# A new order for all instructions of a planned attention and expert kernel, with durations from the trace

## Chip, cores and metric

The kernel runs on one core of a Trainium2 chip. The metric is the device time in microseconds (us) of one execution; the median of several runs is given.

## The reference

A linear attention with a decaying state runs over 4 x 8 heads of 768 steps with 48 channels. Its outputs, taken as 3072 tokens of 384 channels, go through an RMS norm and a gated expert layer.

```python
for t in range(S):                       # attention, per batch and head
    state = alpha[t][:, None] * state + outer(k[t], v[t])
    y[t] = q[t] @ state
rms = sqrt(mean(x * x, axis=-1) + 1e-06)  # x: the 3072 x 384 outputs y
xn = x / rms * rms_g
g, val = xn @ w_gate, xn @ w_val          # 384 x 1536 each
out = (g * sigmoid(g) * val) @ w_out      # 1536 x 384
```

## The kernel before

The 3072 tokens are cut into 24 chunks of 128 (cc counts them; batch b is cc modulo 4). For a chunk, VectorE scans the decays forward and backward (`scan`, L644), with a reciprocal between the two (`rec`, L664), and multiplies k and q by the running products (`kh`, `qh`). TensorE then forms scores (`sc`, for the first four chunks `sc32`), VectorE masks them (`mask`, `near`), TensorE multiplies by v (`yv`, `y32`), sums the state (`u`) and gives the output y. The first four chunks start from no state and have short forms: `kp`, `kb`, `y32`, `ys32`. ScalarE squares y (`sq`, L951), POOL takes the power -1/2 (`pow`, L956), VectorE scales (`x32`, L965), TensorE transposes (`xp`, L972) and takes the rounded half off (`xneg`, L986), and ScalarE writes the two halves of x into tile xT.

Numbers are held as a 16-bit float and its 16-bit remainder, so one product of the experts is three matmuls with K = 128 for each of three parts. A step `mm` (L1152) is 9 matmuls into one PSUM bank. Tokens go in groups of 4, 2, 2, 4, 4, 4 and 4 chunks; for a group, each of 12 blocks of the hidden layer gets two `mm` steps (gate and value), then `silu` (ScalarE), `gate` (VectorE, L1169), `h_hi` (ScalarE, L496) and `h_lo` (VectorE, L1186). The output products are `po` (L1471) for the first five groups, and for the last two a scheme with seven products for eight, in steps of 9 matmuls (L1353), with `snap` (ScalarE, L1388) and `give` (VectorE, L1398 and L1400). The weights arrive as 8-byte words and are put together by `abs`, `shift`, `rest`, `wh` and `wl` (L518 to L540) before their first use.

Near the end a check is made: squares of recorded sums (ScalarE, `1e2`), a sum over partitions by TensorE (`1e3`), comparisons on VectorE (`1e4`), a second sum by TensorE (`1e5`) and a flag written by VectorE (`1e6`, L1654 and L1658). Every engine loads the flag into a register (L1676) and branches on it (L1677): one side is a general form of the kernel, the other issues the last three stores of the output, those of the last chunks, which SP holds back until then.

Nothing is ordered at run time: every step is an operation of a plan (about 1800, numbered as they are made), with an engine, a cost, the operations that it depends on and the buffers that it uses. ORDER lists the numbers in base 36. The planner walks through this list, gives each operation the earliest time by the costs, by its engine and by its inputs, picks the buffer that comes free first, and puts dummy matmuls (`warm`, L1591) where TensorE would wait by its reckoning in the first 45 us. Then all operations are issued in the order of these times, each engine's queue in this order. A transfer is issued by SP in its place of the same list.

Some numbers that are used below: `x`, `10`, `1m`, `1p` scans and `y` the reciprocal of chunks 1 and 2; `f`, `g`, `15` masks; `1r` a `qh`; `3b`, `3c` shift and join of the first weights, `39` their load, `3` the load of chunk 0's v; `j` y32 of chunk 0; `1f` x32 of chunk 1; `2p` ys32, `2r` squares, `2u` transpose and `2w` xneg of chunk 3; `6r` the gate product of block 4; `1dy` the last expert step of TensorE, `1dz` the `give` behind it, `1dv` the one before; `1dw` and `1e0` are SP's places for the last stores, which issue nothing there.

Of the kernel before, what the change touches and what calls it, by code (L numbers as in the profile page):

```python
# [62 lines left out]
COST = dict(
    scan=1.2, rec=0.19, kh=0.605, qh=0.337, kl=0.6, vl=0.47, ql=0.6, gd=0.09, sd=0.28, sl=0.27, mask=0.6,
    al=0.6, st=0.31, ss=0.12, x=0.46, xl=0.53, shift=0.525, rest=0.88, wl=0.87, ob=0.46, oba=0.385,
    dec=0.11, k16=0.62, v16=0.515, q16=0.62, s16=0.26, a16=0.515, sq=0.7, x16=0.52, st0=0.23,
    abs=0.91, odd=0.47, cnt=0.85, wh=0.845, pow=0.6, sc=1.03, scw=0.955, sc32=0.6, yv=0.665, yvw=0.548, y32=1.4, add=0.47, take=0.4, u=0.82, po=1.48, xp=0.46, kp=0.5,
    neg=0.3, hs=1.47, hsh=1.05, hsl=1.2, tw=0.95, ts=1.2, th=0.74, tl=0.87, p7=0.75, snap=0.33, give=0.36, wid=0.75, wneg=0.22, wl2=0.37, rgw=0.7, rgt=0.37, x32=0.53, xb=0.38, ys32=0.82, kb=0.53, near=0.34, xneg=0.22,
)
# [22 lines left out]
6s 45 6t 6o 9v 6x 6p 44 42 ai 6y 6z a3 6e 73 46 4a 6u 4f 47 6q 74 am 4b 75 6k a4 70 76 4c 77 79 an 71 48
4r 7a 7b 78 4d ao 7f 7g aq 7h 7c 9w a5 7l 7d ap 4g 7e 7m 4h 7n 4s 4i 7r 4e 4l 7o 4t 7p 7s ar 4j ay 72 4u
7t 6v 7x 7q 4v 4x 7u 9x 7v 7i as 4w 7y 7z az 4m 7w 4n 21 83 a7 4o au 4k 4p 53 ew 84 a6 b0 4y 80 a9 81 6w
89 85 4z a8 50 4q 5f 51 8a aa 54 86 8b 55 ab aw 56 8f 87 82 59 57 ib e0 ac ic 8g 8h 8c ax b1 52 8l at av
bg 5a ae 8m 5b 8n 88 8d 58 5g b2 5c 7j 8r 8i 5d 5l b4 8j b3 7k 8s b5 8k b6 b7 ad 8t 8o e2 im bh b8 af 8u
b9 5m 5h 8x 5i 8e 5r 5j 8y e1 5e 5k 8z 5n 5o 90 ed e3 5p 5x ex 91 8v dz ee e4 5s 5q 92 8p 5t ef ba 5u 93
e7 e5 5v 8w 94 5z 5y 5w 60 95 bk bb 61 8q 96 bi 62 eg 97 e6 ag eb e8 ah 98 bc ec bd e9 be eh 9b ey bf 9f
ez f0 ej 9c 9d kc ei el 9e 9g f1 9h en ea 99 fb f7 f3 9i f2 f4 j9 id f9 bm ev f5 fc bn f6 bo fd ie 9j ft
ig bs if ek bt em kd bu 9a iq f8 by bp ja ii ih bz c0 bj bv c4 ij c1 lc bl c2 fu jb bq io eo jc bw ir c5  # L100
c6 fa ep fe ca br c3 er eq cb c7 cc bx ik fx cg ip fy ch cd fv ce je jd cm ci jf ff cj il ck cn is fh j8
co c8 fg cs c9 fi cl ct es jo cp in cu fj jg cy fw jh cv cz p5 jm jp p6 ke cw d4 d0 cx d5 fk d6 cq cf jq
da d1 jk fl db et dc d2 cr eu kf dg d7 kh dh di kg jn dm dd kj de d3 ki fm dj dn kk fn fp q5 df dk le d8
do ji it lg dl iu lf fo kr d9 lh dp fq pg jj kl fr ds kp li fs iv dt iw ix k6 lj dq lk iy jr du 9k km dr
lr ph p7 ld dv x3 iz fz j0 dw jl j1 kq g1 p9 g0 ks j2 j4 p8 kn g5 pa js pc g7 pb g6 pd jt pi ra ls gb jv
g2 g8 jx g9 gc gd ju g3 gh ll ge q7 gi gj kt q8 lt ga k7 pj g4 gn lb j3 gk qa gl go gp q6 jw ka gt j5 pk
gm qc gf lu gu jy gv qd jz k8 gq gz j6 gr ln gg gs h0 k0 gw ku gx k2 h5 h1 gy q9 lm h6 h2 mb k9 h3 qb kv
h7 ko sa k1 h8 hb j7 kw k3 kx hc ky kb hd k4 lp hh l0 k5 kz he hi l1 hf pe hg hn lo h9 pf hj l2 pl hp qk
ho h4 pm l3 lq l4 ht hk hq lv rc hr hv l5 hu ha lw l6 hz rd ly lx hw lz l7 i0 hx m1 hl m0 l8 qe hy mc hs
re pn ql m2 l9 q4 i1 md m3 hm qg m4 rb qh sb m5 i2 qf dx la m6 mf m7 i5 rf i3 r4 qm qi rg po m8 m9 i6 me  # L110
ma pp rp pq i7 rh ps ri pr pu w3 rl x4 i8 pt qn sc pv i9 r5 sd se qj pw sl mh r6 rj sf sg mi mj rq mg rn
px ro mn sh r8 si y8 w5 i4 qo ia mp w6 mo sn qq mk w7 qs r7 sj rk mt py sp rm s9 qp mq qr w4 mu w8 mv xe
xf wa mz wb wi w9 mw qt n0 n1 sq mx qu mr x5 n5 ml mm q0 x6 n6 sk n7 ms sr t9 ss sm qv pz z8 n8 nb z9 n2
q1 rr wj n3 my q2 nc nd rs x8 x7 qw qx nh ne so nf rt nj qy ni ru rv rw ng n9 xa nn rx ry wc rz r0 ta xb
np r9 qz x9 no r1 nk n4 tb ya s0 nt r2 yb r3 s1 td yd yc wg nu nv s2 na s3 wh st s4 s5 nz te xg wd we nw
x2 nl yn nq xc o0 sv 13u o1 y9 xi xj nr nm nx yf o5 tc xd yg ye o6 wf 12v o7 za y2 sx ny ob o8 o2 o3 oc
od o4 s6 yo o9 ns oh s7 180 zb 176 oe s8 su oi sz sw q3 xh of oj oa xk zj og wk zc y3 zn sy ok y6 181 wl
182 183 zd on zf zo t0 177 y4 oo 16u 178 ze t1 zp t2 op yp zg 14t 12x wm 12z yj oq wn t3 184 zl wo t4
16x ot 185 12w 12y 16v wq zk t5 wp ou 13v ws 17l t6 zm 16w ov y7 zh wr or zi ol ow t7 om 130 os t8 wt oz
131 wu 107 wv 16y ww p0 zq 17u wx 132 17m zr yk 17n 17c p1 zs yq yh zt ox p2 yi zu yl z7 zv tf 17v 14u  # L120
xl ym 17f wy tg 133 th 13w p3 16z tl 13y 17w 17d 149 zw 170 15s ti 13x tm 13z tn tj y5 wz tr x0 17g to
17o 17h x1 zx ts tt 141 171 tp 142 179 154 140 tx tu 155 14v 15t p4 108 tz 13a 17e zy ty 17p zz 10b 172
17x 109 100 14w 101 u3 102 tq 103 17a u4 u5 13b 16r 14y 13c 17b tk xm tv u0 17q u9 17y 147 14a 173 xo
14x 17z u6 104 ua 148 xq xn ub 13d xp xs uf u7 xr u1 105 14b 16s 10a 17i xt 158 u2 106 ug xu 136 xv uh
u8 143 yr 144 174 ul uc 17r tw ud 14z xw um ui 175 xx xy 150 uj ys ur un 159 yu 17j 15a yt 186 uo us ut
14c 137 up 15b 151 163 15u 16t ux yv 15v yw 152 uq 15w uy 17k yx uz uk 156 10c v3 167 xz 153 187 uu 188
v0 yy y0 v4 145 168 y1 17s v5 164 yz uv z0 v9 ue 169 v1 uw z1 v6 14d z2 157 v7 15x vb va 15z v2 vf vc z3
v8 z4 vg 14f vd 17t ve vh 14e 16a 160 vi 189 165 14g 14h vl 14i vj 18a vk vm 166 14j vn 146 15y 18d vo
z5 z6 vr vp 161 vq 162 14k vs 14l 18b 14m 14n 16b 18c 14p vt 138 16d 16c 139 vu 16e 14o 16f 16g 134 16h
vx 14q 135 vv 14r vw 16i 18e vy 16j 16k 16l vz 16n 16m w0 16o 16p 13e w1 w2 10d 14s 13f 13g 13h 16q 13i  # L130
13j 10e 18f 13k 10f 18g 13l 10j 13m 13n 10g 13o 18l 10k 10l 13q 13p 18t 10s 10m 18u 10t 10u 18m 18v 13r
18w 10y 18n 10v 10p 15c 110 13s 10z 15e 13t 18o 15g 10w oy 15d 10h 117 10n 15i 10i 15f 111 10q 10o 118
112 10r 119 11d 11a 10x 15h 114 11e 11f 18p 115 15j 11g 11b 11m 18q 11h 11c 18r 113 11n 11o 11i 15k 18s
11s 116 11p 18h 11t 11u 11j 121 15l 18i 15m 11q 122 11v 18j 15o 123 15n 18k 11k 127 11r 1e1 11w 124 11l
128 129 11x 125 11y 12g 11z 12a 15p 120 12h 12i 12b 126 15q 12m 12d 15r 12j 12e 12n 12c 12o 12f 12k 18x
12p 18y 12s 12q 18z 190 12l 12t 12r 191 12u 193 192 194 196 195 197 199 198 19a 19b 19c 19f 19d 19e 19h
19i 19l 19j 19k 19m 19o 19n 19p 19q 19r 19u 19s 19t 19v 19z 19w 19g 1a0 19x 1a3 1a1 1a2 1a4 1a7 19y 1a5
1a8 1a9 1ad 1aa 1ab 1ac 1ae 1af 1am 1ag 1aj 1an 1ak 1ao 1as 1ah 1ap 1al 1at 1au 1aq 1b1 1av 1ay 1b2 1b3
1ar 1ai 1az 1b0 1b7 1b4 1b8 1b9 1bg 1ba 1bh 1bi 1bb 1aw 1bm 1ax 1bc 1bj 1bn 1bd 1bk 1bo 1be 1bv 1bf 1bw
1bp 1bl 1bq 1bs 1bx 1c1 1by 1bz 1c2 1c0 1c3 1br 1b5 1bt 1ca 1bu 1c4 1cb 1c7 1cc 1c8 1cg 1cd 1c5 1ce 1c6  # L140
# [1627 lines left out]
```

## Time and profile before

| what | value |
|---|---|
| median of 3 runs | 501.1 us (500.85 to 501.48) |
| span of the profiled execution | 500.0 us |
| its own time | listed by its span alone; 1.1 us less than the median of the runs |
| TensorE, matmul | 491.6 us busy, 98% |
| VectorE | 422.2 us busy, 84% |
| ScalarE | 277.0 us busy, 55% |
| POOL | 25.6 us busy, 5% |
| DMA | 65.22 MB, mean 130 GB/s |

The span reaches from the first to the last instruction of the profiled execution. Busy time counts arithmetic alone: loads into registers, branches and waits are not in it. Matmuls overlap in time, so that their busy times can add up to more than the stretch that they fill. The chain of waits gives 77% of the span to TensorE and 12% to VectorE, VectorE's part nearly all in the first 117 us.

### The profile page before, as it was taken

Reading aid. Unit: us, or ns where it says so; the run is one execution under the profiler, and the core shown is the slowest. Engines: PE = TensorE matmul, PEld = TensorE weight load, DVE = VectorE, ACT = ScalarE, POOL = GpSimd, SP = SyncE. Lnnn points to the kernel's source line nnn. Section 1 sums busy time; section 2 is a strip of 40 time slices with the busy share of each in tenths; the row PEclk is TensorE's granted clock in tenths of the full one; section 3 lists DMA queues with packets and bytes.
Section 4 is the critical chain, followed back from the end, with each engine's and each line's share of the span. In section 5 each row is a group of like instructions: output and inputs, shape, how many; then the busy total and the mean of one; then the engine's idle time right before and its main releaser. Section 6 shows DMA issues by size and latency. Waiting matters only on the chain.

```text
span 500.0 us, 12691 instructions
## 1 busy us (share of the span) xinstructions
PE 491.6 (98%) x5204; PEld 311.3 (62%) x5204; DVE 422.2 (84%) x822; ACT 277.0 (55%) x751; POOL 25.6 (5%) x63
## 2 busy tenths in 40 slices
...
GB/s 326 240 299 244 191 229 208 159 94 246 100 108 182 62 96 192 130 99 17 216 240 294 322 289 206 108 17 49 64 12 21 2 16 18 31 1 1 1 2 83
DMA packets 47042, 65.22 MB, mean 130 GB/s; under 512 B 32641, under 2 KB 39042, under 8 KB 46978
## 3 DMA queue, kind: packets, MB, share of 16 engines
...
q8 instruction: 41, 0.67, 0.5%
q14 instruction: 23, 0.19, 0.1%
HBM read 52.03 MB, written 4.72 MB: 113 GB/s over the span
## 4 chain that ended last, share of the span: by engine, by line
PE 77%; DVE 12%; issue 5%; DMA 2%; POOL 1%; ACT 1%; SPq 0%; DVEq 0%; POOLq 0%; ACTq 0%
PE mm L1152 48%; PE mm_po L1471 14%; PE mm_ab L1353 6%; PE at L751 3%; PE at_d L1353 2%; DVE w L644 2%; PE y L851 2%; PE at L924 1%; DMA raw_o<-w_out 1%; DVE wu_o L532 1%; DVE h L1169 1%; DMA out_dram<-ob 1%; PE y L830 1%; DVE h L1186 1%; DVE wu_i L532 1%
## 5 line engine op out<-in xcount | busy, mean ns | idle before, releaser
L1152 PE MATMUL mm<-xT,wg 128*128 128x512 f16 (+1 forms) x1602 | 287.6, 338 | 0.5 <-DVE h L1169 0.3
L1152 PEld LDWEIGHTS <-wg 128*128 128x128 f16 x1602 | 154.1, 98 | 121.8 <-issue 2.1
L1471 PE MATMUL mm_po<-wo,h 128*128 128x384 f16 x576 | 96.8, 326 | 0.2 <-DVE wo L540 0.2
L1471 PEld LDWEIGHTS <-h 128*128 128x128 f16 x576 | 55.2, 98 | 36.1 <-issue 0.4
L1163 ACT ACTIVATE sl<-mm 128x512 f32<-128x512 f32 (+1 forms) x89 | 45.1, 508 | 54.2 <-PE mm L1152 53.8
L1169 DVE SCALAR_TENSOR_TENSOR h<-mm,sl 128x512 f32<-128x512 f32 (+1 forms) x89 | 51.3, 582 | 14.9 <-PE mm L1152 10.4
L496 ACT ACTIVATE h<-h 128x512 f16<-128x512 f32 (+1 forms) x89 | 45.6, 513 | 32.8 <-DVE h L1169 32.7
L644 DVE TENSOR_TENSOR_SCAN w<-att,seed 112x520 f32<-112x520 f32 x48 | 59.4, 1237 | 2.2 <-DMA att<-att 1.8
L1186 DVE TENSOR_TENSOR h<-h,h 128x512 f16<-128x512 f32 (+1 forms) x89 | 47.4, 546 | 6.0 <-ACT h L496 5.8
L956 POOL TENSOR_TENSOR ss<-ss,mhalf 128x1 f32<-128x1 f32 x24 | 19.7, 820 | 367.4 <-ACT ss L953 303.6
L767 DVE TENSOR_TENSOR at<-at,mask 128x512 f32<-128x512 f32 x40 | 26.9, 691 | 3.7 <-PE at L751 3.7
L878 ACT CAST a<-at 128x512 f16<-128x512 f32 x40 | 22.8, 582 | 12.0 <-DVE at L767 11.8
L881 DVE TENSOR_TENSOR a<-at,a 128x512 f16<-128x512 f32 x40 | 26.7, 682 | 1.0 <-ACT a L878 0.8
L681 DVE TENSOR_TENSOR qp<-att,w 112x256 f32<-112x256 f32 x48 | 19.7, 419 | 0.2
L1353 PEld LDWEIGHTS <-h 128*128 128x128 f16 x216 | 17.9, 98 | 0.6
L751 PEld LDWEIGHTS <-k 48*128 48x128 f16 x480 | 13.4, 94 | 6.7 <-issue 6.3
L496 ACT ACTIVATE q<-qp 112x512 f16<-112x512 f32 x20 | 12.5, 625 | 8.0 <-DVE qp L681 3.4
L751 PE MATMUL at<-q,k 48*128 48x128 f16 x480 | 16.9, 217 | 0.0
L496 ACT ACTIVATION_READ_ACCUMULATOR h<-h 128x1 f32 x89 | 16.8, 189 | 0.0
L688 DVE TENSOR_TENSOR k<-kh,k 112x512 f16<-112x512 f32 x20 | 13.6, 681 | 3.7 <-ACT k L496 3.7
L674 DVE TENSOR_TENSOR kh<-att,w 112x512 f32<-112x512 f32 x24 | 16.4, 685 | 0.2
L851 PEld LDWEIGHTS <-a 128*128 128x128 f16 x368 | 13.6, 96 | 2.7
(200 smaller groups left out, 614.9 us busy)
## 6 DMA issues: line engine op xcount, KB each, us to landing
...
```

The lines of the kernel that those rows point to most:

```text
L496: nc.scalar.activation(dst, src, AF.Copy, scale=scale, accum_out=stat[:rows, col : col + 1])
L644: nc.vector.tensor_tensor_scan(w, x, start.rearrange("r g p c -> r (g p c)"), 0.0, op0=ALU.mult, op1=ALU.add)
L751: nc.tensor.matmul(t["sc"][j][:, p, :], t["k16"][r, x, p, :], t["q16"][r, y, p, :], start=m == 0, stop=m == 2,)
L767: nc.vector.tensor_tensor(t["sc"][j], t["sc"][j], mask.to_broadcast([P, NP, C]), op=ALU.mult)
L851: nc.tensor.matmul(o, a_tile()[:, j, x, p, :], v, start=False, stop=p == NP - 1 and x == 1, skip_group_check=True,)
L881: nc.vector.tensor_tensor(a_tile()[:, j, 1], t["sc"][j], a_tile()[:, j, 0], op=ALU.subtract)
L1152: nc.tensor.matmul(ps[:, :n], wg[:, f, x, j, kk, :], xT[:, y, kk, cs], start=i == 0, stop=i == 3 * NK - 1,)
L1163: nc.scalar.activation(t["sl"][:, :n], t[0][:, :n], AF.Silu, scale=1.0 / (S_X * S_W))
L1169: nc.vector.scalar_tensor_tensor(t["h"][:, :n], t[1][:, :n], S_H / (S_X * S_W), t["sl"][:, :n], op0=ALU.mult, op1=ALU.mult,)
L1186: nc.vector.tensor_tensor(lo, used(t["h"][:, :n]), hi, op=ALU.subtract)
L1353: nc.tensor.matmul(bank(b), left(n, x, p), right(n, y, p), start=begin and p == 0 and m == 0, stop=end and p == n2 - 1 and m == 2, skip_gr ...
L1471: nc.tensor.matmul(t[i][:, :DM], h16_of(g, f)[:, x, ts], wo[:, f // 2, y, f % 2, :], start=f == 0 and m == 0, stop=f == NF - 1 and m == 2,)
```

## The change

The cost tables get new numbers, a table AFTER is added, and the list ORDER is replaced. In the planner's walk, an operation whose input comes from the same engine now starts no earlier than the end of that input plus AFTER: 0.117 us behind an operation of VectorE, 0.175 behind `shift`, none behind `qh` and `near` and on the other engines. No operation is added or removed. In the list below the first line and the last three are shown of each side.

```diff
-    scan=1.2, rec=0.19, kh=0.605, qh=0.337, kl=0.6, vl=0.47, ql=0.6, gd=0.09, sd=0.28, sl=0.27, mask=0.6,
...
+    scan=1.152, rec=0.113, kh=0.602, qh=0.335, kl=0.6, vl=0.467, ql=0.6, gd=0.07, sd=0.267, sl=0.266,
...
+AFTER = dict(PE=0.0, DVE=0.117, ACT=0.0, POOL=0.0, SP=0.0, qh=0.0, near=0.0, shift=0.175)
...
-1 0 2 u 4 3 39 v 1k 7 w 2y 8 9 a b c h d e 29 x i 5 y f 6 g 10 j 3a 3b 3c k l 11 3d 3f 1l 12 17 13 z m
...
-1ch 1ci 1b6 1c9 1cp 1cj 1cq 1cf 1ck 1cm 1cr 1cs 1cl 1cn 1ct 1cv 1co 1cu 1cw 1cy 1cz 1d1 1d0 1e2 1d2 1d3
-1d4 1e3 1d7 1d5 1e4 1cx 1da 1db 1de 1df 1dh 1d6 1dg 1dc 1e5 1dr 1di 1dd 1e6 1a6 1d8 1dj 1d9 1dk 1dn 1dl
-1dm 1do 1dt 1dp 1dq 1du 1ds 1dx 1dv 1dw 1dy 1dz 1e0
+0 1 7 9 2 8 a u b h i c d e 4 x f y g 5 6 39 3a 3b 10 z 3c 3 j k l v 12 11 13 14 3d 3e 15 m n o 17 1k 1m
...
+1cp 1cq 1cr 1cs 1cj 1ck 1cm 1cn 1cf 1ct 1cu 1cl 1cv 1cw 1cx 1bf 1co 1cy 1cz 1d0 1d1 1e1 1e2 1d2 1e3 1d3
+1d4 1d5 1d6 1d7 1da 1d8 1dr 1db 1de 1df 1dg 1dh 1di 1dj 1dk 1dn 1do 1dl 1e4 1dc 1d9 1dd 1a6 1dp 1dq 1dt
+1du 1dm 1dx 1dy 1ds 1dv 1dw 1e5 1dz 1e6 1e0
...
-                t = max(t, d["t"] + d["c"] if d["e"] == e else d["f"])
+                t = max(t, d["t"] + d["c"] + AFTER.get(d["k"], AFTER[e]) if d["e"] == e else d["f"])
```

## Rows read from the trace of the kernel before

**Rows 1.** The page, part 1: busy us of each engine (share of the span) x instructions.
```profile
PE 491.6 (98%) x5204; PEld 311.3 (62%) x5204; DVE 422.2 (84%) x822; ACT 277.0 (55%) x751; POOL 25.6 (5%) x63
```

**Rows 2.** Waits of TensorE: line waited for <- releaser: us in total, times, longest.
```profile
PE mm_x L986 <- ACT xT L980: 0.6, 1, 0.6
PE mm_x L972 <- DVE x L965: 0.3, 1, 0.3
PE mm L1152 <- DVE h L1169: 0.3, 1, 0.3
PE at L924 <- DVE a L881: 0.3, 1, 0.3
```

**Rows 3.** Groups by form: out<-in, shapes, count | busy us, mean ns | idle before.
```profile
L1591 PE MATMUL warm<-minus 128*128 128x512 f16 x33 | 8.1, 380 | 0.0
```

**Rows 4.** Timeline of TensorE: start us, us, what, count.
```profile
14.83 2.76 PE L1591 MATMUL warm<-minus 128*128 128x512 f16 x12
...
28.44 1.16 PE L1152 MATMUL mm<-xT,wg 128*128 128x256 f16 x9
```

**Rows 5.** One 5 us stretch: length, then busy us (count) of each engine.
```profile
20.00:25.00 5.00, 4.95 (x82) 3.13 (x81) 5.00 (x9) 3.52 (x9) 0.55 (x1) 1.00 0.53 185
```

**Rows 6.** Timeline of VectorE in the first 20 us.
```profile
8.04 1.24 DVE L644 TENSOR_TENSOR_SCAN w<-att,seed 112x520 f32<-112x520 f32 x1
9.31 0.21 DVE L664 RECIPROCAL seed<-w 112x8 f32<-112x8 f32 x1
...
10.07 1.23 DVE L644 TENSOR_TENSOR_SCAN w<-att,seed 112x520 f32<-112x520 f32 x1
11.21 0.54 DVE L529 TENSOR_SCALAR wu_i<-raw_i 128x768 int32<-128x768 int32 x1
11.86 0.96 DVE L532 SCALAR_TENSOR_TENSOR wu_i<-raw_i,wu_i 128x768 int32<-128x768 int32 x1
...
18.88 0.55 DVE L529 TENSOR_SCALAR wu_i<-raw_i 128x768 int32<-128x768 int32 x1
19.35 0.42 DVE L681 TENSOR_TENSOR qp<-att,w 112x256 f32<-112x256 f32 x1
```

**Rows 7.** Instructions on tile flag: ns min/median/max, first and last start us (q: sequencer).
```profile
L1676 POOLq TENSOR_LOAD <-flag x1: 690/690/690, 489.0 to 489.0; - x1
L1676 SPq TENSOR_LOAD <-flag x1: 530/530/530, 490.1 to 490.1; - x1
```

**Rows 8.** Instructions of L1677, the branch, columns as in rows 7.
```profile
L1677 POOLq COMPARE_BRANCH  x1: 45/45/45, 489.7 to 489.7; - x1
L1677 POOLq EVENT_SEMAPHORE  x1: 17/17/17, 490.2 to 490.2; - x1
L1677 SPq COMPARE_BRANCH  x1: 53/53/53, 491.0 to 491.0; - x1
```

**Rows 9.** Instructions of L1764, behind the branch, columns as in rows 7.
```profile
L1764 SPq EVENT_SEMAPHORE  x13: 17/28/28, 493.6 to 499.9; - x13
```

**Rows 10.** Timeline of VectorE in the last 12 us.
```profile
488.63 0.15 DVE L1654 TENSOR_SCALAR raw_work<-at_pok 1x1 f32<-1x1 f32 x1
488.81 0.14 DVE L1658 CAST flag<-raw_work 1x1 int32<-1x1 f32 x1
...
495.42 0.36 DVE L1400 SCALAR_TENSOR_TENSOR x<-at_d,sl_o 128x192 f32<-128x192 f32 x1 [1.13 <-PE at_d L1353]
```

**Rows 11.** Timeline of SP, three stretches of the end.
```profile
493.72 0.35 SPq L1404 DMA_DIRECT2D out_dram<-x  x1
...
494.32 0.34 SPq L1404 DMA_DIRECT2D out_dram<-x  x1
...
495.80 0.33 SPq L1404 DMA_DIRECT2D out_dram<-x  x1
```

**Rows 12.** Loads of L518 issued in the first 16 us.
```profile
DMA to landing us min/median/max: 5.8/7.6/9.4
```

**Rows 13.** Stores from tile x issued from 493 us on.
```profile
DMA to landing us min/median/max: 1.6/2.4/3.1
```

More of the change, by code (lines that the diff above doesn't have):

```diff
@@ L63 @@
 COST = dict(
-    scan=1.2, rec=0.19, kh=0.605, qh=0.337, kl=0.6, vl=0.47, ql=0.6, gd=0.09, sd=0.28, sl=0.27, mask=0.6,
[L65 to L68, printed above, removed]
+    scan=1.152, rec=0.113, kh=0.602, qh=0.335, kl=0.6, vl=0.467, ql=0.6, gd=0.07, sd=0.267, sl=0.266,
+    mask=0.598, al=0.598, st=0.264, ss=0.12, x=0.468, xl=0.527, shift=0.48, rest=0.869, wl=0.867, ob=0.46,
+    oba=0.386, dec=0.096, k16=0.614, v16=0.508, q16=0.614, s16=0.242, a16=0.475, sq=0.83, x16=0.515, st0=0.211,
+    abs=0.895, odd=0.469, cnt=0.83, wh=0.83, pow=0.6, sc=0.981, scw=0.949, sc32=0.532, yv=0.606, yvw=0.545,
+    y32=1.439, add=0.466, take=0.372, u=0.817, po=1.463, xp=0.45, kp=0.479, neg=0.3, hs=1.466, hsh=1.055,
+    hsl=1.142, tw=0.867, ts=1.196, th=0.725, tl=0.869, p7=0.743, snap=0.25, give=0.28, wid=0.67, wneg=0.165,
+    wl2=0.362, rgw=0.84, rgt=0.376, x32=0.51, xb=0.376, ys32=0.85, kb=0.53, near=0.3, xneg=0.17,
 )
 IN_COST = {
-    4: (1.954, 0.5, 0.61, 0.63), 3: (1.47, 0.39, 0.47, 0.52), 2: (1.003, 0.28, 0.34, 0.4),
-    1: (0.52, 0.17, 0.21, 0.28),
+    4: (1.943, 0.489, 0.602, 0.613), 3: (1.463, 0.386, 0.467, 0.51), 2: (0.982, 0.264, 0.333, 0.4),
+    1: (0.51, 0.17, 0.2, 0.28),
 }
@@ L92 @@
[L92 to L140, printed above, removed]
-1ch 1ci 1b6 1c9 1cp 1cj 1cq 1cf 1ck 1cm 1cr 1cs 1cl 1cn 1ct 1cv 1co 1cu 1cw 1cy 1cz 1d1 1d0 1e2 1d2 1d3
@@ L142 @@
-1d4 1e3 1d7 1d5 1e4 1cx 1da 1db 1de 1df 1dh 1d6 1dg 1dc 1e5 1dr 1di 1dd 1e6 1a6 1d8 1dj 1d9 1dk 1dn 1dl
-1dm 1do 1dt 1dp 1dq 1du 1ds 1dx 1dv 1dw 1dy 1dz 1e0
+0 1 7 9 2 8 a u b h i c d e 4 x f y g 5 6 39 3a 3b 10 z 3c 3 j k l v 12 11 13 14 3d 3e 15 m n o 17 1k 1m
+w p q 1n 18 1o 16 1p 2y 30 r 2z 19 1a s 1b 29 t 1c 1r 1q 1s 1t 31 33 2b 1u 1w 1d 1e 2c 1v 34 36 2e 1x 38
+1f 1l 3f 3g 3h 32 35 37 2f 2g 2h 2d 1g 1h 3i 9l 9n 1y 1z 1i 1j 2i 2j 20 2a 3j 3k 9p 22 23 9o 2k a0 3l 3n
+a1 24 63 2l 64 65 9q 3r 21 3t 2m 3m 3s 69 6b 25 aj 26 2n 2o 3o 3p 9s 9t 66 67 43 3u 3v 9r 6a 6c 6d 3q al
@@ new lines @@
+27 28 6f 6h 2p 2r 2s 6g 6l 6i 3w 9u 2t 6e 3x 44 45 9m 6m 6n am 6o ew 6j an 6k ay 3z 46 2u 2v 6r 6t 2w 2x
+6s 6u 6x 6y ao 3y 47 6v 48 9y 6w 6z a2 6p 73 74 aq 70 71 75 40 9v 6q 79 7b 7a 7f 4r 4t 76 2q 9w 72 9z 4s
+77 7g 7h 4u a3 7l 68 7i 78 41 42 7c a4 a6 49 4b 7j 7k 4v a5 4a 7n 4c 4w 7m 7o 4d 4e ap 7r 7t ar 4f 4h 7s
+7x 7y 4g 7p 7q 4i 7z 9x 7u 4l 4n a7 7d 7e a8 4m 4o 80 4j as 83 85 4k 84 89 ai ak au a9 aa ab 4x 59 av az
+4z aw ax 4y at 8a 81 b0 4p 4q 8b 7v b1 ae 50 86 ac ad 51 5b 8f 5a 8h ex dy dz e0 e2 5c 82 52 b2 b3 5d 8g
@@ new lines @@
+8i 8l 8m 87 53 bg 8j 8n 55 7w b4 88 54 56 8o 8r 8s b5 b7 b6 b8 5f 8k 8c j9 bh 57 f7 58 8t 8u b9 8p 5h 5g
+ed 5i 5e bk 5l 5m af 5n ee 8x 5j 8d 5o 8q 8y 5r 8v 8z 90 5k 91 ag 8e 5t 92 5p 5q e1 93 5s 5u e3 5x 5z ef
+5v 5w 5y 60 ba bb bc 61 e4 e7 62 bi e5 e6 eb ib 94 95 8w eg 96 97 98 9d e8 ev ah ec eh ey f8 ez bd be f1
+f0 f3 f2 f4 e9 ei bf f5 9b ej el fb fc fd 9e id ie ig f9 f6 ih ii 9f 9c 9g 9h 9i ea 99 9j if ft bm ek bo
+lc 9a bn bs bp 9k bj ic bu bt ij bv by bq bw en em bz fe bx c0 jb ik io c4 c6 eo fa fu fx er c5 c1 jd c2
@@ new lines @@
+c7 br jc ep ca cc cb cg ch c8 c3 fv ip je bl jo cd ce ff jf jp eq ci cj jg ck cf iq fg fw ji cm cn fh cs
+co fi cp fk ct fj fl cu cl jh c9 cy cq d0 es kc il j8 cv cw ke et jq fm fn cz d1 fy d2 ir kf kh cx cr d4
+d6 d5 d7 is da db dc p5 ld fo dg di im kg dh it d3 ki ja fp d8 dm dj dk jk fq dd de kr kj kk ks le d9 q5
+iu iv ix iw dl eu df iy jm j0 kt dn iz do dp ds dq kp kl ln fr jj in jn lg j1 j2 jr kq j4 lf lr km lh lj
+lk li k6 dt js jt jv ju du dv fs kd fz g0 dw jl j3 j5 kn g1 g5 g7 p7 p8 ls pa jx g6 gb g8 lp j6 jw jy lo
@@ new lines @@
+g9 p9 ga gd gc ge jz k0 k7 gh gj gi ll pk g2 pb ka k2 gf g3 lq dx pc pd gn go ku k1 k3 k8 ko k9 q7 gp gk
+gg gl q6 sa lb kv kw gq ky kx kz q9 kb gt gu gv lm gz g4 j7 gw q8 gm h0 h5 lt lu h1 h2 h3 l1 l0 k4 h4 h6
+h7 h8 l2 l3 l4 ra gx gy gr qa hb l5 mb gs l6 hd qg hc he hf hh hj l7 qb l8 pi lv lx lz lw l9 la hi hn qe
+hp ho pl pm m1 ht qk qc qd ly m0 h9 ha pn hq hr sb p6 ql rc mc hk rd md hg mf m2 hs hu hv hz re hw pe pf
+pj i0 i1 qi q4 m3 m4 hx hy hl hm m5 m7 m6 m8 rf rg m9 dr rh ri po pq i2 i3 sc k5 pg pp rn sd ro qf ps sf
@@ new lines @@
+qj pr sh si qm qn me pu qh i5 mg sg i6 i7 i8 i9 w3 ma mh mi mj se rj ph pt mn mp y8 pv r4 w5 w6 rk w7 rb
+w8 r5 r6 pw px wi mk py pz mo r8 mq mr x3 r7 mt q0 q1 rp rq rr mv w9 q2 qo wa r9 qp qq qs qr mu mz ms wb
+qu qt x4 x5 sj sk ia ml n0 n1 n2 qv qw qx rs wg qy n3 s9 x6 mm x8 n5 qz n6 n4 r0 n7 sl n8 n9 rt ru nb mw
+sn rw sm nd wj wh mx sp sq x7 rl sr wk xa ry xb nc nh rv x9 rx ss ni rm ya yc nj r1 t9 ta rz s0 my ne nk
+nf tb r2 s1 q3 w4 nn no yn np td so na xi wl xc xd s2 nl nm s3 we yb te nt nv yd yf st sv su xe wc nu xg
@@ new lines @@
+sw sx nq wd 13u nz nr o1 r3 o0 o5 13v xf yg nw wf s5 s4 sz sy t0 ye ns o2 o3 z8 za zb xj zd nx o6 o7 s6
+s7 t1 o4 y9 y2 x2 y3 xh y6 tc yo ob o8 o9 y4 t2 ny y5 oc 176 xk 12v ng t3 od oe t4 of wm ze zh t5 t6 og
+wo oh oi oj oa ok zc zn zo zp on oo wn zi 177 107 zf yj zg t7 wp z9 14t t8 wq ws zl wr wt op 12x zm 12z
+183 xl 12y s8 wu y7 wv zq 130 132 131 oq or ww wx os zr zs 133 wy yh zj zt yl ym yi ot ou ov zu zw yk i4
+13w wz 13y 13x 13a 13z ow oz ol zv p0 p1 zx 140 zk zy 141 z7 142 om 14v 14w 145 184 185 x0 149 108 p2
```

24 lines of the change are left out of this document (20 added, 4 removed).

## The prediction

> **What bounds the kernel now.** The page came first: TensorE is busy for 491.6 of 500.0 us [rows 1], so an order can win only where TensorE waits, where it runs dummy matmuls in place of waiting, or at the two ends. The waits of TensorE came next: after the start four of 0.3 us or more, 0.6 + 0.3 + 0.3 + 0.3 = 1.5 us in all [rows 2]. The dummies (`warm`, L1591) are 33 [rows 3], and a run of 12 lasts 2.76 us [rows 4], so 0.23 us each and 7.6 us together. The first real product of the experts starts at 28.44 us [rows 4]; before that TensorE waits for VectorE, which is busy for 5.00 of the 5.00 us from 20 us on [rows 5]. So the start is VectorE's, the middle TensorE's. The end I read last, row by row: which engine loads the flag when, and when SP may issue the last stores [rows 7 to 11].
>
> **The change part by part.** I read the numbers of ORDER as the plan's operations, in base 36. Since the planner's times on one engine only grow, the order on an engine is the order in the list. TensorE's order hardly changes (of 378 steps 169 keep their place, none moves by more than 12); VectorE's and ScalarE's change a good deal. COST, IN_COST and AFTER issue nothing: they act through which buffer a tile gets and how many dummies are put in.
>
> *Neighbours on VectorE.* A scan started at 8.04 and the reciprocal that reads its result at 9.31, 1.27 us later; the scan of 10.07 has an independent shift behind it at 11.21, 1.14 us later. A shift with its own join behind it takes 11.86 - 11.21 = 0.65 us, one with another operation behind it 19.35 - 18.88 = 0.47 us [rows 6]. So a dependent neighbour costs 0.13 us behind a scan and 0.18 behind a shift. Ahead of `1f` (the scaled x of chunk 1, on the way to the first product) both orders hold the same 33 VectorE steps; the new one parts `x y`, `3b 3c` and `1p 1r`: 0.13 + 0.18 + 0.13 = 0.44 us. Some of it is eaten, since `15` now stands ahead of scan `1m` and must wait for its scores. I take 0.3 us of a possible 0 to 0.44.
>
> [...]
>
> *The fourth chunk's x.* `2u` (transpose) is followed by `2w`, which must wait until ScalarE has rounded the half that it subtracts: 0.6 us lost at L986 [rows 2]. The new order puts the product `6r` (1.1 us, as the first one [rows 4]) between them. I count 0.6 won; it is 0 if the weights for `6r` are late, whose last step stands three VectorE steps later than before.
>
> *The other waits.* VectorE gets ahead: of its first 200 steps 24 had a dependent neighbour before and 11 have one now. I count the 0.3 us at L1152 (behind `h`) and the 0.3 at L924 (behind `a`) as gone; the 0.3 at L972 stays, because the step of VectorE that it waits for moves by one place only and `2p`, whose sums that needs, comes one product later. The front is 0.3 + 0.6 + 0.3 + 0.3 = 1.5 us. Its bounds: a gain of 3 (all four waits, the 0.44, and 1 us of dummies), a loss of 0.5 for waits that rows of another order can't show.
>
> *Queues.* On SP the load of the first weights (`39`) goes ahead of chunk 0's v (`3`). That load takes 5.8 us from an issue at 3.0 [rows 12], so v lands some tenths behind 8.8; its reader `j` stands behind `g`, which VectorE ends when it starts the scan of 10.07 [rows 6]: hidden, by about 1 us. Other loads on SP move by up to 23 places; POOL's memsets `1e1` move to right ahead of `1e2`, with two products of TensorE between that and `1e3`, which waits for them. Both I count at 0, inside the 0.5.
>
> *The end.* Here the list adds a wait. Before, `1e5` (the check's last matmul) and `1e6` (the flag) stand well ahead of the last expert steps: the flag is written at 488.81 [rows 10], POOL loads it at 489.0 and SP, behind its own stores, at 490.1 [rows 7]; SP branches at 491.0 [rows 8] and its first record behind the branch is at 493.6 [rows 9]. It then can issue each of the last three stores as its data come: 493.72, 494.32 and 495.80 [rows 11], the last right behind the result of 495.42 [rows 10]. All of load and branch lies beside TensorE's last products. In the new list the end is `1dw 1e5 1dz 1e6 1e0`: `1e5` stands behind `1dy`, the last product, and `1e6` behind `1dz`, the last result on VectorE. Nothing is left to hide load and branch, and the three stores, queued behind the branch on SP, wait for both. What comes then: TensorE's last product ends 0.1 us sooner (the check's matmul left its stream), the result runs from 495.3 to 495.7, the two small steps take 0.3 (488.63 to 488.95 [rows 10]), SP loads at 496.0. From SP's load to its first store there are 493.72 - 490.1 = 3.6 us, to the second 0.6 more, to the third 0.6 again: 500.8. From the third store's issue to the end of the span there were 500.0 - 495.80 = 4.2 us. Sum: 505.0, so 5.0 us are added. The lower bound takes the quickest landing of these stores in place of the slowest, 1.6 for 3.1 us [rows 13]: 3.5 added. The upper one lets the three stores, now 1.2 us apart in all, slow each other by 0.3: 5.3. I take 5.0, the rows' own.
>
> *Sum:* 500.0 - 1.5 + 5.0 = 503.5 us of span. The median of the runs, 501.1, stands 1.1 above the profiled span; that part outside of it I leave unchanged: 504.6 us.
>
> **The rivals.**
> 1. *SP's branch is short.* POOL's branch at 489.7 has its next record at 490.2, 0.5 us later [rows 8], where SP's took 2.6. Should SP be that quick in the new kernel, 2.1 of the 5.0 go: 500.0 - 1.5 + 2.9 + 1.1 = 502.5. Against it: SP runs the same code to the same target. [...]
> 2. *The start shrinks far more* (the other side). Of the dummies 25 come behind the first real matmul, 5.7 us; if the new VectorE order let the first product start earlier by all that they fill, and the 1.5 us of waits went too, it would be 500.0 - 7.2 + 5.0 + 1.1 = 498.9. It decides for faster from a gain of 6.0, with the waits gone a first product at 23.9 us. For it: TensorE does stand without work there. Against it: VectorE was full and has the same 33 steps to do.
> 3. *The flag isn't late after all*: the change doesn't do at the end what the list says, or the stores don't stand behind the branch. Then 500.0 - 1.5 + 1.1 = 499.6. Against it: SP's records behind the branch begin 0.1 us ahead of the first of these stores.
> 4. *The new order brings waits of its own in front*, as at `2r`, the squares of chunk 3, which now stand behind one more `silu` on ScalarE, so that x comes late by one product, 1.1 us; twice that, with nothing won: 500.0 + 2.2 + 5.0 + 1.1 = 508.3.
>
> **How the numbers follow.** A measurement of this kernel can't tell less than 0.2%, 1.0 us, from no change: faster is below 500.1, slower above 502.1. Forecast 504.6 with 0.76; rival 1 0.08, rival 2 0.04, rival 3 0.06, rival 4 0.06. Rivals 2 and 3 are faster: 0.10. Of rival 1 and the forecast's lower edge (a front of 3 and an end of 3.5: 501.6) I put 0.08 within 0.2%; slower 0.82. The range takes in the forecast's bounds, 501.6 and 500.0 + 0.5 + 5.3 + 1.1 = 506.9, and with them rival 1: 501.6 to 506.9, which leaves out rivals 2 to 4.
>
> **What would show it.** Right: the flag's CAST is VectorE's last step; SP loads it within 0.3 us and its first store follows 3.6 us later; the last result is written some 1.5 us sooner, and the span ends some 9.5 us behind its start where it was 4.6 (500.0 - 495.42); the wait at L986 is gone; a scan with a reciprocal right behind it has become rare. Wrong: the last store issued right behind the last result, SP past its branch in 0.5 us, a first product before 26 us, or waits of TensorE that add up to more than 1.5 us.

## The result, and the profile after

| what | before | after |
|---|---|---|
| median of 6 runs each | 501.01 us (500.24 to 502.16) | 503.84 us (503.09 to 505.18) |
| ratio of the runs | 1 | 1.0052, 95% interval 1.0035 to 1.0070 |
| span of the profiled execution | 500.0 us | 501.4 us (its own time 503.09) |
| last result on VectorE starts | 495.42 us | 493.49 us |
| from there to the end of the span | 4.6 us | 7.9 us |

The change makes the kernel slower by 2.8 us, 0.5%. Both halves of the forecast are in the last two lines: the work ends 1.9 us sooner, and what comes behind it takes 3.3 us longer.

TensorE's busy time, to be held against [rows 1], and its waits (us in total, times, longest), against [rows 2]:

```profile
PE 490.3 (98%) x5203; PEld 311.5 (62%) x5203; DVE 420.6 (84%) x822; ACT 277.8 (55%) x751; POOL 24.2 (5%) x63
```

```profile
PE mm_ab L1356 <- DVE x L1403: 0.4, 1, 0.4
PE mm_x L975 <- DVE x L968: 0.3, 1, 0.3
PE mm L1155 <- DVE h L1172: 0.3, 1, 0.3
```

The waits at L986 (L989 now) and L924 are gone. That for x32 stays at 0.3, as foretold. The 0.3 at L1155 is another one, near 78 us: the old one, at 47.53, is gone. New is 0.4 at L1356 (484 us): a `give` now stands between two products that write the bank which it reads, and the second product waits for it.

TensorE's timeline in front, first of the kernel before, then of the changed one (start us, us, what, count):

```profile
29.52 0.69 PE L761 MATMUL at<-qp,kh 48*64 48x64 f32 x32
30.15 2.14 PE L1152 MATMUL mm<-xT,wg 128*128 128x256 f16 x18
...
40.85 0.55 PE L972 MATMUL mm_x<-one,x 128*128 128x128 f32 x3 [0.33 <-DVE x L965]
41.97 0.32 PE L986 MATMUL mm_x<-xT,minus 128*128 128x384 f16 x1 [0.57 <-ACT xT L980]
42.13 5.07 PE L1152 MATMUL mm<-xT,wg 128*128 128x256 f16 x45
47.53 0.27 PE L1152 MATMUL mm<-xT,wg 128*128 128x256 f16 x1 [0.33 <-DVE h L1169]
```

```profile
28.81 1.16 PE L1155 MATMUL mm<-xT,wg 128*128 128x256 f16 x9
29.81 0.55 PE L891 MATMUL at<-one,kh 112*128 112x112 f32 x4
30.19 2.13 PE L1155 MATMUL mm<-xT,wg 128*128 128x256 f16 x18
...
40.72 0.55 PE L975 MATMUL mm_x<-one,x 128*128 128x128 f32 x3 [0.30 <-DVE x L968]
41.11 1.15 PE L1155 MATMUL mm<-xT,wg 128*128 128x256 f16 x9
42.09 0.33 PE L989 MATMUL mm_x<-xT,minus 128*128 128x384 f16 x1
42.25 5.51 PE L1155 MATMUL mm<-xT,wg 128*128 128x256 f16 x49
```

The first product stands at 28.81 us where [rows 4] had 28.44, which looks like a loss of 0.4 us. It is none: before, the scores of chunk 3 (`2i`, the row of 29.52) came behind that product, and now they come ahead of it, while `kp` (`2l`, the row of 29.81) went the other way. At the second product the two kernels are level: 30.15 and 30.19. At the x of chunk 3, before took 1.28 us from the transpose (40.85) to the next row of products (42.13); now it is 1.53 with the product `6r` inside (0.98), so 0.73 us are won.

VectorE in front, against [rows 6]:

```profile
7.95 1.24 DVE L647 TENSOR_TENSOR_SCAN w<-att,seed 112x520 f32<-112x520 f32 x1
9.11 0.42 DVE L780 TENSOR_TENSOR a<-at,near 128x256 f32<-128x256 f32 x1
...
9.85 0.55 DVE L532 TENSOR_SCALAR wu_i<-raw_i 128x768 int32<-128x768 int32 x1
10.32 1.22 DVE L647 TENSOR_TENSOR_SCAN w<-att,seed 112x520 f32<-112x520 f32 x1
...
15.24 0.42 DVE L780 TENSOR_TENSOR a<-at,near 128x256 f32<-128x256 f32 x1 [0.70 <-PE at L764]
```

The neighbours are parted as planned: a mask, not the reciprocal, stands behind the scan of 7.95 (1.16 us later), a scan behind the shift of 9.85 (0.47). But 0.70 us are lost at 15.24, where the mask `15` waits for scores.

The end: VectorE's last result and the flag behind it, SP's load of the flag, its branch, its records behind it, its three stores, and the packets of the kind `instruction`, by queue, from 495.5 to 496.5 us; against [rows 7 to 11]:

```profile
493.49 0.36 DVE L1403 SCALAR_TENSOR_TENSOR x<-at_d,sl_o 128x192 f32<-128x192 f32 x1 [1.13 <-PE at_d L1356]
...
493.94 0.14 DVE L1661 CAST flag<-raw_work 1x1 int32<-1x1 f32 x1
```

```profile
L1679 SPq TENSOR_LOAD <-flag x1: 478/478/478, 494.1 to 494.1; - x1
```

```profile
L1680 SPq COMPARE_BRANCH  x1: 45/45/45, 494.7 to 494.7; - x1
```

```profile
L1767 SPq EVENT_SEMAPHORE  x13: 17/28/28, 495.2 to 501.3; - x13
```

```profile
495.31 0.34 SPq L1407 DMA_DIRECT2D out_dram<-x  x1
...
495.87 1.84 SPq L1407 DMA_DIRECT2D out_dram<-x  x1
...
498.58 0.34 SPq L1407 DMA_DIRECT2D out_dram<-x  x1
```

```profile
q14 instruction: 4, 0.03, 11.8%
q8 instruction: 1, 0.02, 9.4%
```

The flag is the last thing that VectorE writes. SP loads it at 494.1, branches at 494.7 and is on the other side at 495.2, only 0.5 us later, where it took 2.6 before. Yet the stall was not saved, it fell further back: the second store, 0.56 us behind the first, takes 1.84 us to issue, and the third comes only at 498.58, 3.3 us behind the first. Meanwhile code is fetched: five packets, read as one fetch each, from 495.7 to 495.9 us. The profile does not name their engines; since all five engines branch between 494.6 and 494.7 us, they are read as one for each.

### The profile page after: what moved, and what is told of

It is laid out like the page before. It is cut to its first block, busy times and chain, and to the rows that moved or that the text cites. A ratio compares the mean times of both kernels' runs of the same rounds, so it can differ in the third digit from the quotient of the medians.

```text
span 501.4 us, 12683 instructions
## 1 busy us (share of the span) xinstructions
PE 490.3 (98%) x5203; PEld 311.5 (62%) x5203; DVE 420.6 (84%) x822; ACT 277.8 (55%) x751; POOL 24.2 (5%) x63
## 4 chain that ended last, share of the span: by engine, by line
PE 81%; DVE 9%; issue 2%; DMA 1%; ACT 1%; DVEq 0%; SPq 0%; ACTq 0%
PE mm L1155 47%; PE mm_po L1474 18%; PE mm_ab L1356 6%; PE at L754 3%; PE at_d L1356 2%; PE y L854 2%; PE at L927 1%; DVE h L1172 1%; DVE wu_i L535 1%; DVE wg L543 1%; PE y L833 1%; DMA raw_i<-w_in 1%; DVE h L1189 1%; DVE w L647 1%; DVE wu_o L535 1%
## 5 line engine op out<-in xcount | busy, mean ns | idle before, releaser
L1155 PE MATMUL mm<-xT,wg 128*128 128x512 f16 (+1 forms) x1602 | 287.4, 338 | 0.3 <-DVE h L1172 0.3
L1155 PEld LDWEIGHTS <-wg 128*128 128x128 f16 x1602 | 154.2, 98 | 120.4 <-issue 0.6
L499 ACT ACTIVATE h<-h 128x256 f16<-128x256 f32 (+1 forms) x89 | 45.8, 515 | 36.9 <-DVE h L1172 36.5
L959 POOL TENSOR_TENSOR ss<-ss,mhalf 128x1 f32<-128x1 f32 x24 | 18.3, 762 | 389.4 <-ACT ss L956 359.6
L1356 PEld LDWEIGHTS <-h 128*128 128x128 f16 x216 | 17.9, 98 | 0.8 <-issue 0.6
L854 PE MATMUL y<-v,a 128*128 128x96 f16 (+1 forms) x368 | 14.5, 189 | 0.0
L999 DVE SCALAR_TENSOR_TENSOR x<-x,ss,x 128x384 f16<-128x384 f32 x20 | 12.1, 607 | 2.5 <-ACT x L996 2.5
```

Of the source, the lines that this page charges most:

```text
L499: nc.scalar.activation(dst, src, AF.Copy, scale=scale, accum_out=stat[:rows, col : col + 1])
L854: nc.tensor.matmul(o, a_tile()[:, j, x, p, :], v, start=False, stop=p == NP - 1 and x == 1, skip_group_check=True,)
L1155: nc.tensor.matmul(ps[:, :n], wg[:, f, x, j, kk, :], xT[:, y, kk, cs], start=i == 0, stop=i == 3 * NK - 1,)
L1356: nc.tensor.matmul(bank(b), left(n, x, p), right(n, y, p), start=begin and p == 0 and m == 0, stop=end and p == n2 - 1 and m == 2, skip_gr ...
```

## The experiments

Each was timed against the kernel before in the same session, whose median there was 501.6 us (29 runs) for the first four, 501.7 (35) for the next four, and 501.35 (9) for the last three. Times stood 1.7 to 1.8 us above their own spans in all of them, for either list.

**The flag early in the new list** (`after_flag_early`).

```diff
-... 1di 1dj 1dk 1dn 1do 1dl 1e4 1dc 1d9 ... 1dw 1e5 1dz 1e6 1e0
+... 1di 1e4 1dj 1dk 1e5 1dn 1do 1dl 1dc 1e6 1d9 ... 1dw 1dz 1e0
```

> The changed kernel, with the check's last steps moved ahead again in the list (1e4 before 1dj, 1e5 before 1dn, 1e6 behind 1dc); all else as changed. Theory, the late flag costs the whole loss: the last result is still written at about 493.5 us, and the span ends some 4.6 us later, at 498.1, as before the change; median 499.2 to 499.8, 0.3% below the kernel before. Rival, the loss sits in front or outside of the span (1.7 us now, 1.1 before): it stays above 502.

Measured: 500.58 us (12 runs), ratio 0.9973 (0.9959 to 0.9987). VectorE's flag and last result, SP's branch and its three stores:

```profile
490.73 0.14 DVE L1661 CAST flag<-raw_work 1x1 int32<-1x1 f32 x1
...
495.11 0.36 DVE L1403 SCALAR_TENSOR_TENSOR x<-at_d,sl_o 128x192 f32<-128x192 f32 x1 [1.13 <-PE at_d L1356]
```

```profile
L1680 SPq COMPARE_BRANCH  x1: 53/53/53, 491.8 to 491.8; - x1
```

```profile
492.53 0.35 SPq L1407 DMA_DIRECT2D out_dram<-x  x1
...
494.62 0.33 SPq L1407 DMA_DIRECT2D out_dram<-x  x1
...
495.50 0.96 SPq L1407 DMA_DIRECT2D out_dram<-x  x1
```

The branch lies beside TensorE's last products again, the third store follows the last result by 0.4 us, and the end comes 3.7 us behind that result. The last result itself came at 495.11 us and not at 493.5, since this execution's first product came 1.1 us later (29.93), and the median lies 0.8 us above the range expected. Against the kernel before of its session it is 0.3% less, as expected: the late flag is the whole loss, and without it the new list beats both kernels.

**The flag late in the old list** (`before_flag_late`).

```diff
-... 1dh 1d6 1dg 1dc 1e5 1dr 1di 1dd 1e6 1a6 ... 1dy 1dz 1e0
+... 1dh 1d6 1dg 1dc 1dr 1di 1dd 1a6 ... 1dy 1e5 1dz 1e6 1e0
```

> The kernel before, with only 1e5 moved behind 1dy and 1e6 behind 1dz. Theory, the late flag alone: the last result at 495.3 us as before, SP loads the flag some 0.6 us later, and the end comes 3.3 to 5.0 us later; median 504.3 to 506.0. Rival, the place of the flag doesn't matter: 501.0.

Measured: 505.66 us (6 runs), ratio 1.0073 (1.0054 to 1.0092): two moved steps lose 3.7 us by the ratio, 4.0 by the medians. SP's branch and its records behind it:

```profile
L1677 SPq COMPARE_BRANCH  x1: 45/45/45, 496.7 to 496.7; - x1
```

```profile
L1764 SPq EVENT_SEMAPHORE  x13: 17/28/28, 500.2 to 504.2; - x13
```

Here the stall does stand at the branch, 3.5 us of it, and the three stores then follow within 1.2 us.

**One store held, not three** (`after_one_store_held`): in the new list two of the last three stores are issued as their data come, ahead of the branch.

```diff
-if end and q: last_store.append(lambda: store(1)) ...
+op("SP", 0.4, lambda: store(1), [c21, t["c22"]], [obs[1]])
-if end: last_store.append(lambda: store(0, 1, 2)) ...
+if end and q: last_store.append(lambda: store(0, 1, 2)) ...
+elif end: op("SP", 0.4, lambda: store(0, 1, 2), [c12, t["c11"]], [obs[0]])
```

> The changed kernel, but two of the three last stores are issued ahead of the branch; one waits for the flag. The flag stays late. Theory, the price is the row of three stores on SP behind the branch: the one store is issued some 1.2 us behind SP's load of the flag (495.3 in place of 498.6) and the median is 500.5 (499.5 to 501). Rival, the price is the branch itself (2.6 us as in the kernel before): the store at 497.4, median 502.5 to 503.5.

Measured: 503.81 us (12 runs), ratio 1.0045 (1.0032 to 1.0057), the same as the changed kernel within the intervals. SP's records around the branch and the one store:

```profile
L1678 SPq EVENT_SEMAPHORE  x7: 17/17/17, 499.9 to 500.4; - x7
...
L1678 SPq COMPARE_BRANCH  x1: 45/45/45, 495.7 to 495.7; - x1
```

```profile
496.39 0.34 SPq L1407 DMA_DIRECT2D out_dram<-x  x1
```

The store goes out 0.7 us behind the branch, and then SP stands until 499.90. So the row of three stores is not the price, and the rival's store at 497.4 did not come either. What the trace has in this gap is the fetch of code, five fetches from 496.7 to 497.0 us; that SP waits for its own among them is read from the times, not shown by a releaser.

**The old list with the new costs** (`before_list_new_costs`): the changed kernel with the old ORDER.

> The old list with the new cost tables and AFTER. Theory, the list does it all and the tables only choose buffers and the number of dummies: 501.0, within 0.7 us of the kernel before. Rival, the tables bring the gain in front (1.9 us): 499.1.

Measured: 501.70 us (12 runs), ratio 0.9999 (0.9986 to 1.0012). The tables by themselves do nothing that can be told from 0; the interval leaves room for 0.7 us.

**The end of the old list** (`after_old_end`): the new list up to `1d4`, then the old one's order.

```diff
-1d4 1d5 1d6 1d7 1da 1d8 1dr 1db 1de 1df ... 1e4 1dc ... 1e5 1dz 1e6 1e0
+1d4 1d7 1d5 1e4 1da 1db 1de 1df 1dh 1d6 1dg 1dc 1e5 1dr 1di 1dd 1e6 1a6 1d8 ... 1dz 1e0
```

> The new list up to 1d4, and behind it the steps in the order in which the old list has them (so 1e4 stands ahead of 1d6, 1d8 and 1dr, and the flag comes early). Theory: the end of the new list costs twice, by the late flag and by the wait of 0.4 us of TensorE for a give (L1403) near 484 us. That wait is there because the give 1d8 stands between the products 1da and 1db, which write the bank that it reads. With the old end both are gone: no wait of TensorE at L1356 over 0.2 us, the last give 0.3 to 0.5 us sooner than with the flag alone moved forward, an end of 3.7 to 4.6 us behind it, and 499.4 to 500.4 us against 501.2 to 501.6 of the kernel before (ratio 0.995 to 0.998). Rival: the wait of 0.4 us comes from the products' own order and stays, or it is paid at another place; then the time is that of the flag moved forward alone, 500.6 (ratio 0.997 to 0.999).

Measured: 500.46 us (12 runs), ratio 0.9976 (0.9961 to 0.9991). The rival was right: no better than the flag alone, since the wait was paid at another place, two steps of 9 products later (ahead of `1df`, where it was ahead of `1db`):

```profile
485.06 0.41 PE L1356 MATMUL mm_ab<-v_T,att_S 128*128 128x192 f16 x3
485.92 0.24 PE L1356 MATMUL mm_ab<-v_T,w_S 128*128 128x192 f16 x1 [0.45 <-DVE x L1403]
```

**The mask behind the scan** (`after_old_end_15`).

```diff
-... 3d 3e 15 m n o 17 1k 1m w ...
+... 3d 3e m n o 17 1k 1m 15 w ...
```

> The kernel with the old end, and the mask 15 (near of chunk 1) moved back behind the scan 1m, where the old list has it. Theory: in the new list VectorE stands 0.70 us ahead of 15 for the scores of TensorE, and this eats the 0.44 us won at the neighbours. With 15 behind the scan the wait goes, x32 of chunk 1 starts 0.4 to 0.7 us sooner when counted from the first scan's start (20.85 us in the changed kernel, so 20.1 to 20.4), the first product of the experts comes 0.4 to 0.7 us sooner, and the whole is 0.4 to 0.7 us shorter than the kernel with the old end alone. Rival: the first product waits for something else (scores, transposes or the load behind the first scan), VectorE only waits at another place: first product and whole within 0.2 us of the kernel with the old end.

VectorE's mask `15`, and x32 of chunk 1:

```profile
15.71 0.39 DVE L780 TENSOR_TENSOR a<-at,near 128x256 f32<-128x256 f32 x1
...
23.87 0.59 DVE L968 SCALAR_TENSOR_TENSOR x<-y,ss,rg 128x384 f32<-128x384 f32 x1
```

The wait of 0.70 us is gone; x32 starts 20.21 us behind the first scan (3.66), as the theory had it, and the first product comes 0.5 us sooner (28.37 against 28.88). But with `15` where the new list has it one of six executions started x32 after 20.47 us and its first product at 28.47, so a single profile can't show the gain. The median is 500.30 us (12 runs), ratio 0.9978 (0.9964 to 0.9992): against the kernel with the old end no gain can be told. The wait is gone; whether anything is won stays open.

**`6r` alone** (`before_6r_first`).

```diff
-2u 6n 2v al 49 6j 2w dy 6r 2x
+2u 6n 2v 6r al 49 6j 2w dy 2x
```

> The kernel before, with nothing but the gate product 6r of block 4 moved ahead of 2w (xneg of chunk 3). Theory: the wait of 0.6 us at L986 goes, and what is won there stays to the end: 0.5 to 0.8 us less (ratio 0.9984 to 0.999), as in the changed kernel, where the step behind came 0.85 us sooner. Rival: it is given back within some us, since VectorE or ScalarE bring the next block no sooner; then a wait of TensorE of some 0.5 us shows behind 43 us and the time is within 0.2 us of the kernel before.

TensorE around it:

```profile
42.56 1.14 PE L1152 MATMUL mm<-xT,wg 128*128 128x256 f16 x9
43.54 0.33 PE L986 MATMUL mm_x<-xT,minus 128*128 128x384 f16 x1
44.44 2.81 PE L1152 MATMUL mm<-xT,wg 128*128 128x256 f16 x24 [0.57 <-ACT xT L989]
```

The product fills the wait ahead of L986, and the next product then waits 0.57 us for ScalarE's other half of x: the wait has moved by one step, as the rival said. The time says otherwise by a little: 501.23 us (12 runs), ratio 0.9982 (0.9969 to 0.9996). From the first product to the last result this execution took 467.12 us, the two of the kernel before 466.98 and 466.34. Whether `6r` alone wins anything stays open; in the new list the same place has no second wait.

**The three pairs parted in the old list** (`before_neighbours`).

```diff
-... 29 x i 5 y f 6 g 10 j 3a 3b 3c ... p 1p q 19 r 1r 2z 30 ...
+... 29 x f i 5 y 6 g j 3a 3b 10 3c ... p 1p q 19 r 30 1r 2z ...
```

> The kernel before, with three pairs of VectorE parted: the mask f between scan x and reciprocal y, the shift 3b ahead of scan 10 (which so stands between shift and join), and the shift 30 between scan 1p and 1r. Theory: each parted pair wins its gap (0.13 + 0.18 + 0.13 = 0.44 us): x32 of chunk 1 starts 20.1 us behind the first scan's start (20.54 in the kernel before), and the first product 0.3 to 0.44 us sooner; the time 0.2 to 0.44 us less. Rival 1: the gap isn't tied to the neighbour, the start stays at 20.5 us. Rival 2: VectorE wins it and loses it at the next wait for TensorE (the masks behind scores that come later), so that first product and time stay within 0.2 us, or the masks wait so long that it is slower by up to 0.5 us.

VectorE's x32 of chunk 1, here and in the old list with the late flag, where no pair is parted:

```profile
24.83 0.62 DVE L965 SCALAR_TENSOR_TENSOR x<-y,ss,rg 128x384 f32<-128x384 f32 x1 [0.38 <-POOL ss L956]
```

```profile
24.72 0.62 DVE L965 SCALAR_TENSOR_TENSOR x<-y,ss,rg 128x384 f32<-128x384 f32 x1 [0.38 <-POOL ss L956]
```

The pairs are parted, but x32 starts 21.25 us behind the first scan (3.58), not 20.1, and waits 0.38 us for POOL's `pow`. This wait does not come from the parting: it stands in the same size in the old list with the late flag, whose front is unchanged, and x32 starts there 21.08 us behind the first scan (20.54 in both profiles of the kernel before). The time is 502.53 us (12 runs), ratio 1.0009 (0.9994 to 1.0023). So no gain is seen, and at most 0.3 us could hide in the interval. That VectorE loses at the next wait what it won (rival 2) fits this, but is not shown.

**The flag halfway** (`after_flag_mid`).

```diff
-1dt 1du 1dm 1dx 1dy 1ds 1dv 1dw 1e5 1dz 1e6 1e0
+1dt 1du 1e5 1dm 1dx 1dy 1ds 1dv 1e6 1dw 1dz 1e0
```

> The new list with 1e5 moved ahead by two products, behind 1du, and 1e6 behind the give 1dv: the flag is written some 1.6 us sooner (at about 492.3 us where the changed kernel has 493.94), still 1.2 us ahead of the last give, so behind most of TensorE's work. Theory: what a late flag costs is paid one for one: load, branch, code fetch and the three stores follow the flag by about 7.5 us, so 1.6 us sooner gives 1.3 to 1.8 us less, 502.0 to 502.6 (ratio to the kernel before 1.001 to 1.003). Rival: the fetch waits until all five engines branch, and TensorE and VectorE branch only at the end of their own queues; then the stores stay where they are, and the time is within 0.5 us of the changed kernel, 503.3 to 504.1 (ratio 1.0035 to 1.005).

Measured: 502.82 us (5 runs), ratio 1.0035 (1.0021 to 1.0048), between the theory's range and the rival's. The flag, and SP's first two stores behind the branch:

```profile
492.87 0.14 DVE L1661 CAST flag<-raw_work 1x1 int32<-1x1 f32 x1
```

```profile
494.57 0.35 SPq L1407 DMA_DIRECT2D out_dram<-x  x1
...
497.55 0.33 SPq L1407 DMA_DIRECT2D out_dram<-x  x1
```

By the clock of the two profiles the flag came 1.1 us sooner than in the changed kernel, but this execution ran later (last result at 494.14 us, there at 493.49). Counted from the last result, the flag came 1.7 us sooner (1.27 us ahead of it, there 0.45 behind it), and the end 0.95 us sooner (6.96 us behind it, there 7.91; 8.13 in the changed kernel's second profile). So some 1.0 to 1.2 of 1.7 us are won, and not one for one; SP again stalls between its first store and its second (3.0 us). The rival's rule falls by the kernel before: there SP goes on at 493.6 us, ahead of TensorE's branch (494.3) and VectorE's (496.0).

**Both kernels a second time** (`after_again`, `before_again`), unchanged.

> The changed kernel unchanged, for a second profile. Theory: the first product of the experts (28.81 us in the first profile) differs by up to 1 us from execution to execution, since the masks and x32 wait for transfers and scores; from the first product to the last give it takes the same 464.7 us within 0.5. Rival: both repeat within 0.2 us, and so the 0.4 us between the first products of the two kernels is the list's.

> The kernel before unchanged, for a second profile. Theory: its first product (28.44 us in the first profile) comes at 28.4 to 29.6 us, and from there to the last give it takes 467.0 us within 0.5, 2.3 us more than the changed kernel. Rival: 28.44 repeats within 0.2 us; then the new list loses 0.4 us at the start. SP's stretch from the branch to the first store is 2.6 us again by the one reading; if it is anything from 0.5 to 3.5 us, the length of the code fetch is a matter of the execution.

First products: 28.47 and 28.48 us, so the 0.4 us of the first pair is within what one execution differs from the next; over all profiles the second product comes at 29.9 to 31.3 us with the new list and at 30.2 to 31.4 with the old one. From the first product to the last result it took 465.20 and 466.34 us; the gap is 1.1 here where the first pair had 2.3, so the 2.3 did not repeat, and 0.3 of each is owed to the swapped scores (from first to second product 1.71 us before, 1.38 after). SP's records behind its branch of 490.4, in the kernel before:

```profile
L1764 SPq EVENT_SEMAPHORE  x13: 17/28/28, 493.0 to 498.9; - x13
```

That is 2.6 us again (493.0), and in the changed kernel 0.5 again, with the third store 3.5 us behind the first (499.02, 495.49). Where the stall falls belongs to the program, not to the execution.

## Why the prediction was right, and where its steps failed

The forecast was 504.6 us, the time is 503.84. The gain in front had the right size, the loss at the end the right cause. All places counted on TensorE's own steps, from the second expert product (us until the step named starts; ahead of each the same steps lie in both lists, but for `1e5` of some 0.1 us ahead of `1dy`). The old list's executions are the kernel before twice, the late flag and the new costs; the new list's are the changed kernel twice and the flag halfway:

| step | old list, 4 executions | new list, 3 executions | means apart |
|---|---|---|---|
| 6g, block 2 | 7.13 to 7.26 | 7.11 | 0.11 |
| 7m, block 4, second half | 24.12 to 24.45 | 23.07 to 23.11 | 1.26 |
| c4, group 1 | 87.35 to 87.99 | 85.80 to 85.91 | 1.82 |
| 10d, group 5 | 326.86 to 327.49 | 325.15 to 325.67 | 1.79 |
| 1da, ahead of the new wait | 453.81 to 454.44 | 452.09 to 452.61 | 1.80 |
| last product 1dy | 463.68 to 464.32 | 462.35 to 462.87 | 1.28 |

So 1.8 us are won by the first 120 us and stay to the end but for 0.5, which the new wait at L1356 takes. Foretold were 1.5. With the two other kernels that have the new list's front (flag early, one store held) the means at `10d`, `1da` and `1dy` are 1.7, 1.7 and 1.2 apart. The size is in part luck: one term of the sum is not to be seen, and of the 0.6 us between `7m` and `c4` the rows trace only L924's share.

1. *Neighbours on VectorE*, 0.3 us: not shown. The pairs were parted and each ran quicker, by 0.11 us and 0.18, but `15` lost 0.70 us (0.33 in the changed kernel's second profile). At the second product the first pair of kernels is level, and in the second pair the new list leads by 0.3 us (29.85 against 30.19); with either list that product wanders by more than 1 us from execution to execution, so that 0.3 can't be told from 0. The sentence on `15` ("some of it is eaten") should have been worked out: a mask ahead of a scan of 1.15 us brings it to its scores by as much sooner.
2. *The fourth chunk's x*, 0.6 us: right, and 0.73 by the rows. That `6r` alone does it is not shown.
3. *The other waits*: L1152's 0.3 us gone at 47.53, x32's 0.3 stayed. L924's wait comes and goes with the old list (0.3, 0.5, 0.2 and 0.5 us in four of its six profiles, none in the other two) and stands in no profile of the new one, so it was won, by 0.25 us in the mean of the six. Missed was the new one at the end.
4. *Queues*, at 0: nothing in the runs speaks against it.
5. *The end*, +5.0 us: the mechanism was right, and the two exchanges of the flag's place show it from both sides (0.8% between the early and the late flag in the new list, 4.0 us; 3.7 us in the old). From the start of the last result to the end 9.5 us were foretold, and 7.9 and 8.1 came. The term is 3.3 us in the first pair of profiles, 4.0 in the second and 4.2 between the old list with the late flag and without. From SP's load to the third store 4.5 us were needed where 4.8 were foretold, but the shape was another: branch 0.5, first store, then the stall. The part that was mis-sized is the one from the third store to the end: 2.8 us, in both profiles, where [rows 11] with the span had given 4.2; the kernel before has 3.7 in its second profile. The lower bound had taken the quick landing and came to 2.7.
6. *The part outside the span*: 1.7 us, not 1.1; the 1.1 had set the median beside the span of an execution that is not among the three runs. This and an end that was too dear nearly cancel, which is luck: to the profiled 503.09 us it is 504.6 - 0.3 (result sooner) - 0.1 (load) - 0.3 (stores) - 1.4 (landing) + 0.6.

*Rival 1* (SP past its branch in 0.5 us) was named with a sign that did occur, and the gain that it promised did not. The sign was ill chosen, since it looked at the branch and not at the stall behind it. With the old list SP stands at the branch, 2.6 us in both profiles of the kernel before and 3.5 us with the flag late; with the new list it first goes on, 0.5 to 0.6 us behind the branch and by one store or two, and stands then, so that the changed kernel's third store comes 3.3 us behind its first (with the old end no such stand shows). In none of these profiles does SP's next record come sooner than 0.5 us behind its branch, and none names what SP stands for there. Rivals 2 and 3 fell: the second product comes 0.3 us sooner at most in the two pairs, and the flag was late. Rival 4 came as 0.4 us at another place, not as 2.2.
